# Attention and ELU feed-forward on one core: v by even and odd columns, w_in in eight loads over 128 partitions, and another order of all steps

## The chip, the core and the metric

The kernel runs on one core of one Trainium2 chip. The metric is the device time of one execution in microseconds. Three runs of the kernel before took 332.55, 333.47 and 333.83 us; the median is 333.47 us.

## The reference

Attention over 8 batches, 8 heads, 576 tokens and 64 dimensions, with 16 beacon keys and values ahead of the causal ones, and then a feed-forward layer on the 4,608 tokens (512 to 2,048 to 512) with an ELU between its two products. All inputs and the output are float32.

```python
k_all = np.concatenate([beacon_k, k], axis=2)
v_all = np.concatenate([beacon_v, v], axis=2)
scores = scale * np.matmul(q, k_all.transpose(0, 1, 3, 2))   # causal ones masked, beacons always seen
a = np.exp(scores - scores.max(-1, keepdims=True))
a /= a.sum(-1, keepdims=True) + 1e-09
x = np.matmul(a, v_all)         # then heads side by side: (4608, 512)
h = x @ w_in
g = np.where(h > 0.0, h, np.exp(np.minimum(h, 0.0)) - 1.0)
return g @ w_out
```

## The kernel before

All engines run an order that is written out by hand: the string handed to `run` (L789 to L912) is a list of some 1,500 words such as `S.1.4`, and each word calls one step, which emits its instructions. Within an engine the instructions keep the order of the words; between engines only the data they pass and the buffers they share hold them back, by semaphores. So a step that waits holds up all later steps of its engine. The words are a plan made elsewhere; in the kernel stand only its result and the pools whose buffers it has to respect.

A word's first number is the batch for attention steps and the token tile for feed-forward steps. Tiles 0 and 1 are the first 512 tokens in halves of 256, tiles 2 to 9 have 512 tokens each. The steps, with their engine:

- `warm` and `wm` (PE): dummy matmuls of 512 and 128 columns.
- `lq`, `lv`, `wi`, `wo`, `lk` (POOL): loads of q and k (L136), v (L144 and L149), w_in (L161), w_out (L165), and of q and k of later batches to scratch in DRAM (L759). They change the type on the way and are issued by POOL. The program has eight semaphores for POOL's loads and gives them out in turn, so that a load waits for the landing of the eighth load before it.
- `lp` (POOL, L775 and L776): fills the beacon columns and the padding of a key buffer for batches 3 and later. These buffers are the ones from which batches 1 and 2 are transposed. `lt` (SP, L766) is the DMA transpose from scratch for the same batches.
- `T` (PE, L265): transposes of q and k for batches 0 to 2 into PSUM; `cq` (DVE) and `ck` (ACT) copy them out (L278); `cb` (DVE) puts in the beacon keys.
- `S` (PE, L319): scores of 512 columns (416 for batch 0) and two heads; `x` (ACT, L334): their exp into `et`; `m` (DVE, L339): the causal mask; `D` (DVE, L392): sums for the denominators.
- `L` (PE, L376 and L418): column sums of the exps, with a matrix of ones; `n` (ACT, L433 and L436): Ln and Exp that make the reciprocals; `W` (PE, L376): exps times v; `M` (DVE, L470, L480 and L487): product of both into `xT`, the input of the feed-forward layer.
- `F` (PE, L510): first product for 128 of the 2,048 columns (256 for tiles 0 and 1); `e` (ACT, L520), `u` (ACT, L526, or DVE with `.v`, L528), `k` (DVE, L538), or `r` and `g` (DVE): the ELU into `gt`.
- `G` (PE, L559) with `o` and `s`: second product of tiles 0 and 1. From tile 2 on the second product is made with seven products of halves in place of eight: `wt` and `Z` (DVE, L580) make the sums, `Q` (PE, L626) a part of the 112 matmuls of a tile, `J` (ACT or DVE) takes them out and SP stores them. Tiles 8 and 9 make 12 of the 16 parts of the first product in the same way (`H`, `X`, `P`, `K`, `E`, `U`, `V`).

PSUM has three tags of two buffers each: `hps` (F, P, and the transposes of batch 0), `S` (scores, transposes of batches 1 and 2, L and W, two banks each), and `ops` (G, Q, and L and W of batch 0's first 256 queries). A step that takes a buffer waits until the buffer's last reader is done.

In `quad` (L367 and on) the weights of a W matmul are 32 columns of one head of v, and four heads stand side by side in the 128 columns of PE. `half` says which 32 of the 64 columns. So partition 32*i + d of `xT` holds, for head i of a group of four, column d (half 0) or 32 + d (half 1), and w_in must have its rows in the same order. That is why `load_wi` (L157) makes one load for each head: 32 partitions, two rows each, 1,024 columns; eight loads for each half of the columns.

Of the kernel before, what the change touches and what calls it, by code (L numbers as in the profile page):

```python
# [17 lines left out]
def kernel(  # L18
# [135 lines left out]
    wi_v = moe_w_in.rearrange("(g i t d) f -> i d g t f", i=4, t=2, d=32)  # L154
    wo_v = moe_w_out.rearrange("(f p) m -> p f m", p=P)

    def load_wi(c):  # L157
        f_ = slice(DF // 2 * c, DF // 2 * (c + 1))
        for g in range(2):
            for i in range(4):  # L160
                nc.gpsimd.dma_start(  # L161
                    out=w_in16[32 * i:32 * (i + 1), 2 * g:2 * g + 2, f_], in_=wi_v[i, :, g, :, f_])
# [204 lines left out]
    def quad(b, g, qa, qe, t, half, first):  # L367


        v16 = None if half is None else vt[b]  # L370
        pcs = [(j, max(a, qa), min(e, qe), c + max(a, qa) - a) for (j, a, e, c) in lays[b]
               if max(a, qa) < min(e, qe)]
        for n, (j, a, e, c) in enumerate(pcs):
            for i in range(4):
# [1 line left out]
                nc.tensor.matmul(  # L376
                    out=t[32 * i:32 * (i + 1), a - qa:e - qa],
                    lhsT=ones[0:kc[j], :] if half is None else v16[0:kc[j], j, h, 32 * half:32 * (half + 1)],
                    rhs=et(b, p)[0:kc[j], i % 2, c:c + e - a],
                    start=(first and n == 0), stop=(n == len(pcs) - 1), skip_group_check=True)  # L380
# [415 lines left out]
    m.0.3.2 x.0.2.1 S.0.3.1 m.0.0.0 x.0.3.1 m.0.3.0 cb.1.2 lq.1.0.0.4 S.0.0.3 x.0.0.3 L.0.A
    T.1.0.0 n.0.A cq.1.0.0 cb.1.3 T.1.1.0 ck.1.1.0 wm.4 m.0.0.3 S.1.2 lv.0.2 lv.0.0.1 W.0.A.1
    M.0.A.1 x.1.2 S.1.1 x.1.1 W.0.A.0 M.0.A.0 S.0.3.3 x.0.3.3 S.0.2.2 wi.0 F.0.2 x.0.2.2 S.1.5
    S.1.0 m.0.1.2 e.0.2 m.0.2.2 u.0.2 k.0.2 x.1.5 x.1.0 m.0.0.2 lv.0.3.4 F.0.0 m.0.3.3 F.0.1
    cb.2.0 e.0.1 u.0.1.v k.0.1 L.0.B n.0.B W.0.B.0 M.0.B.0 e.0.0 W.0.B.1 M.0.B.1 u.0.0 k.0.0  # L800
    F.0.3 e.0.3 S.1.4 u.0.3.v k.0.3 x.1.4 wi.1 F.0.4 e.0.4 S.1.3 x.1.3 F.1.1 e.1.1 lq.1.0.4.8
    u.1.1 cb.2.1 T.1.2.0 T.1.3.0 u.0.4.v k.0.4 cq.1.3.0 F.0.5 m.1.1.0 ck.1.2.0 e.0.5 F.1.7
    u.0.5.v k.1.1 e.1.7 u.1.7.v k.1.7 S.1.8 x.1.8 S.1.6 x.1.6 wo.0 G.0.1.0 F.0.6 e.0.6 u.0.6.v
    k.0.6 S.1.7 x.1.7 F.1.4 e.1.4 S.1.11 u.1.4.v x.1.11 F.1.5 e.1.5 k.1.4 S.1.12 x.1.12 S.1.9
    x.1.9 wo.2 u.1.5.v k.1.5 F.1.3 S.1.10 F.1.2 lq.2.0.4.8 T.2.2.0 m.1.0.0 x.1.10 cq.2.2.0
    lq.2.0.0.4 m.1.1.1 m.1.0.1 cb.2.2 e.1.3 T.2.1.0 ck.2.1.0 G.0.0.0 wo.1 u.1.3 T.2.3.0 m.1.3.0
    m.1.2.1 T.2.0.0 ck.2.0.0 cq.2.3.0 lv.1.0.1 G.0.0.1 F.0.7 lk.3.1 S.2.1 e.1.2 H.1.1 m.1.3.1
# [133 lines left out]
```

## Time and profile before

| what | value |
|---|---|
| median of three runs | 333.47 us |
| span of the profiled execution, first to last instruction | 331.3 us |
| granted TensorE clock | 0.998 |
| PE, DVE, ACT busy | 97%, 88%, 83% of the span |
| POOL busy | 27%, nearly all in the first 200 us |
| loads of w_in | 16 of 128 KB, median 5.5 us from issue to landing |
| DMA issues by POOL, SP and ACT | 94, 60 and 5 |

The profile is that of one execution; its span is 2.2 us under the median of the runs, which measure a little more than from the first to the last instruction. PE busy is the time with a matmul somewhere in PE; as matmuls overlap, a busy PE need not be at its peak. KB of a load are those that it writes, after the change of type. "Idle before" is the time that an engine sat idle ahead of an instruction, with what ended it.

### The profile page before, as it was taken

To read this page: it belongs to the slowest core of one execution; us is meant where nothing else is said; L and a number is where in the kernel's file an instruction comes from. 1 tells how busy PE (TensorE), PEld (TensorE's weight loads), DVE (VectorE), ACT (ScalarE), POOL (GpSimd) and SP (SyncE) were. 2 spreads that over 40 slices of the span, in tenths; PEclk is the share of its full clock that TensorE was granted. 3 is DMA by queue.
4 is the path that set the end of the run, shared out by engine and by line. 5 is a ranking of instruction groups with operands and counts; after the bars stand their busy time and mean duration, and the time that the engine had idled before them with its cause. 6 is when DMAs were issued, how large, how long until landed. Compare 5 with 4: busy or idle time off the path is not lost.

```text
span 331.3 us, 8764 instructions
## 1 busy us (share of the span) xinstructions
PE 322.5 (97%) x3576; PEld 208.3 (63%) x3576; DVE 291.8 (88%) x614; ACT 274.9 (83%) x446; POOL 88.3 (27%) x117
## 2 busy tenths in 40 slices
PE   8889999999999999999999999999999999999995
PEld 4657765544446565655665665556656788788784
DVE  3866888989998999999999789999999999999962
ACT  1898998699999998998898789996889687798730
POOL 8888266664008805000830050000000000000000
PEclk9999999999999999999999999999999999999999
DMA  9999999999989998952999098101100011011112
GB/s 114 172 169 182 199 191 172 160 148 156 164 193 69 172 164 135 97 117 60 104 192 153 3 110 133 33 0 34 66 32 3 33 65 34 32 65 34 64 66 95
DMA packets 129113, 34.66 MB, mean 105 GB/s; under 512 B 112944, under 2 KB 127536, under 8 KB 129072
## 3 DMA queue, kind: packets, MB, share of 16 engines
q0 software_dynamic: 94944, 18.49, 67.9%
q1 hardware_dynamic: 33408, 15.34, 20.8%
q8 instruction: 28, 0.46, 0.6%
q10 hardware_dynamic: 720, 0.26, 0.3%
q14 instruction: 13, 0.11, 0.1%
HBM read 37.22 MB, written 15.34 MB: 159 GB/s over the span
## 4 chain that ended last, share of the span: by engine, by line
PE 80%; DMA 10%; POOL 4%; ACT 2%; DVE 1%; issue 1%; DVEq 0%; POOLq 0%
PE hps L510 27%; PE ops L626 27%; DMA v<-in_v_dram 6%; PE sc L319 6%; PE ut L376 6%; PE hps L696 6%; PE ops L559 4%; DMA w_out<-in_moe_w_out_dram 3%; PE sx L626 2%; PE lt L376 1%; POOL qst L136 1%; POOL kst L136 1%; ACT et L334 1%; PE lt L418 1%; POOL v L149 1%
## 5 line engine op out<-in xcount | busy, mean ns | idle before, releaser
L510 PE MATMUL hps<-xT,w_in 128*128 128x512 f16 (+1 forms) x544 | 118.6, 355 | 0.3 <-DVE gt L550 0.2
L334 ACT ACTIVATE et<-sc 128x1024 f16<-128x1024 f32 (+2 forms) x114 | 103.6, 979 | 10.9 <-PE sc L319 10.8
L520 ACT ACTIVATE e<-hps 128x512 f32<-128x512 f32 x120 | 73.2, 617 | 18.9 <-PE hps L510 17.8
L626 PEld LDWEIGHTS <-gt 128*128 128x128 f16 x768 | 73.4, 98 | 19.9 <-issue 3.7
L538 DVE SCALAR_TENSOR_TENSOR gt<-e,r 128x512 f16<-128x512 f32 x112 | 75.4, 684 | 5.7 <-ACT r L526 5.0
L510 PEld LDWEIGHTS <-w_in 128*128 128x128 f16 x544 | 50.6, 98 | 41.9 <-issue 3.9
L526 ACT ACTIVATE r<-hps 128x512 f16<-128x512 f32 x88 | 54.3, 619 | 0.0
L626 PE MATMUL ops<-w_out,gt 128*128 128x256 f16 x368 | 48.0, 273 | 0.0
L626 PE MATMUL ops<-wt,gt 128*128 128x256 f16 x352 | 47.3, 273 | 0.0
L149 POOL DMA_DIRECT2D v<-in_v_dram x40 | 34.7, 914 | 10.6 <-DMA scr<-in_q_dram 3.6
L339 DVE TENSOR_TENSOR et<-et,triu 128x512 f16<-128x512 f16 (+4 forms) x108 | 31.6, 331 | 2.1 <-ACT et L334 2.1
L580 DVE TENSOR_TENSOR gt<-gt 128x1024 f16<-128x1024 f16 x48 | 32.2, 683 | 0.6 <-PE ops L626 0.3
L376 PEld LDWEIGHTS <-v 128*32 128x32 f16 (+1 forms) x800 | 17.4, 96 | 11.6 <-issue 4.2
L392 DVE TENSOR_TENSOR qk<-qk,et 128x672 f16<-128x672 f16 (+2 forms) x66 | 23.3, 367 | 0.5
L376 PE MATMUL ut<-et,v 128*32 128x464 f16 (+3 forms) x560 | 21.3, 296 | 0.0
L144 POOL DMA_DIRECT2D v<-in_beacon_v_dram x8 | 4.8, 595 | 61.8 <-PE lt L376 48.6
L528 DVE TENSOR_SCALAR r<-hps 128x512 f16<-128x512 f32 x24 | 16.4, 685 | 3.1 <-ACT e L520 2.8
L470 DVE TENSOR_TENSOR xT<-ut,rl 128x672 f16<-128x672 f32 (+12 forms) x26 | 16.4, 669 | 1.2 <-PE ut L376 0.7
L642 DVE TENSOR_TENSOR osb<-ops,sm 128x512 f32<-128x512 f32 x23 | 15.7, 682 | 1.0 <-PE ops L626 1.0
L559 PE MATMUL ops<-w_out,gt 128*128 128x512 f16 x64 | 16.4, 381 | 0.0
L735 DVE SCALAR_TENSOR_TENSOR gt<-e,r 128x512 f16<-128x512 f32 x24 | 15.9, 681 | 0.0
L706 ACT COPY kst<-hps 128x512 f32<-128x512 f32 x18 | 10.6, 588 | 5.9 <-PE hps L696 5.8
(113 smaller groups left out, 417.9 us busy)
## 6 DMA issues: line engine op xcount, KB each, us to landing
out_dram<-osb SPq DMA_DIRECT2D x35, 256.0 KB, 2.4
v<-in_v_dram POOLq DMA_DIRECT2D x24, 128.0 KB, 8.4
scr<-in_k_dram POOLq DMA_DIRECT2D x5, 576.0 KB, 12.8
scr<-in_q_dram POOLq DMA_DIRECT2D x5, 576.0 KB, 12.6
w_in<-in_moe_w_in_dram POOLq DMA_DIRECT2D x16, 128.0 KB, 5.5
w_out<-in_moe_w_out_dram POOLq DMA_DIRECT2D x4, 512.0 KB, 10.4
qst<-in_q_dram POOLq DMA_DIRECT2D x4, 288.0 KB, 9.4
kst<-in_k_dram POOLq DMA_DIRECT2D x4, 288.0 KB, 10.0
```

Source lines behind the costliest of these rows:

```text
L149: nc.gpsimd.dma_start(out=vt[b][r0:r0 + n, j, :, :], in_=v[b, :, ilo[j]:ilo[j] + n, :].rearrange("h s d -> s h d"),)
L334: nc.scalar.activation(out=ets[b, d][:, :, a - EC2 * d:e - EC2 * d], in_=sc[b, g][:, :, a - c0:e - c0], func=AFT.Exp, bias=0.0, scale=SCALE)
L339: nc.vector.tensor_tensor(out=o, in0=o, in1=i, op=ALU.mult)
L376: nc.tensor.matmul(out=t[32 * i:32 * (i + 1), a - qa:e - qa], lhsT=ones[0:kc[j], :] if half is None else v16[0:kc[j], j, h, 32 * half:32 * ...
L392: (nc.vector if eng == "v" else nc.gpsimd).tensor_tensor(out=o, in0=t[0:rows, :, a:e] if n == 0 else o, in1=t[0:rows, :, col:col + e - a], ...
L510: nc.tensor.matmul(out=h[:, n_, :], lhsT=w_in16[:, cc, P * fc:P * (fc + 1)], rhs=xt[k][:, cc, a - TT * k:e - TT * k], start=(cc == 0), sto ...
L520: nc.scalar.activation(out=eb[t, i], in_=flat(hp[t, i]), func=AFT.Exp, bias=0.0, scale=1.0)
L526: nc.scalar.activation(out=rb[t, i], in_=flat(hp[t, i]), func=AFT.Relu, bias=0.0, scale=1.0)
L538: nc.vector.scalar_tensor_tensor(out=half(t, i), in0=eb[t, i], scalar=1.0, in1=rb[t, i], op0=ALU.subtract, op1=ALU.min)
L559: nc.tensor.matmul(out=ob[t, tb_], lhsT=gt[:, fc, P * tb_:P * (tb_ + 1)], rhs=w_out16[:, fc, :], start=(fc == 0), stop=(fc == NFC - 1))
L580: (nc.vector if eng == "v" else nc.gpsimd).tensor_tensor(out=o_, in0=a_, in1=b_, op=op_)
L626: nc.tensor.matmul(out=xy[t, n_][:, qd, :], lhsT=lw[:, P * qd:P * (qd + 1)], rhs=wt_[:, c, :], start=(first and c == 0 and (qd == 0 or (t, ...
```

## The change

Three things are changed, and nothing else.

1. `half` now picks the even or the odd columns of v's head (every second element of a row of 64) and not the first or the last 32. Partition 32*i + d of `xT` then holds columns 2d and 2d + 1 of head i.
2. w_in's rows are then in the order in which they lie in memory, two rows for each partition, and one load fills 128 partitions: 128 x 2 x 512, 256 KB. `wi.c` loads a quarter of the 2,048 columns in two loads, and `wi.0` to `wi.3` take the place of `wi.0` and `wi.1`: eight loads in place of sixteen.
3. The string has the same words (but for `wi.2` and `wi.3`) in another order, on all engines. `P` takes its PSUM buffers at whichever of its phases comes first.

```diff
-    wi_v = moe_w_in.rearrange("(g i t d) f -> i d g t f", i=4, t=2, d=32)
+    wi_v = moe_w_in.rearrange("(g p t) f -> g p t f", g=2, t=2)
...
     def load_wi(c):
-        f_ = slice(DF // 2 * c, DF // 2 * (c + 1))
+        f_ = slice(DF // 4 * c, DF // 4 * (c + 1))
         for g in range(2):
-            for i in range(4):
-                nc.gpsimd.dma_start(
-                    out=w_in16[32 * i:32 * (i + 1), 2 * g:2 * g + 2, f_], in_=wi_v[i, :, g, :, f_])
+            nc.gpsimd.dma_start(out=w_in16[:, 2 * g:2 * g + 2, f_], in_=wi_v[g, :, :, f_])
...
-                    lhsT=ones[0:kc[j], :] if half is None else v16[0:kc[j], j, h, 32 * half:32 * (half + 1)],
+                    lhsT=ones[0:kc[j], :] if half is None else v16[0:kc[j], j, h, half:D:2],
...
-        if ph == 0:
+        if (t, g, 0) not in hx:
```

The order of the words up to the first steps of batch 2, engine by engine, where the prediction speaks of it:

```diff
 POOL
-lq.0.0.0.4 lq.0.1.0.4 ident lq.0.0.4.8 lq.0.1.4.8 tri lq.1.0.0.4 lv.0.2 lv.0.0.1 wi.0 lv.0.3.4 wi.1 lq.1.0.4.8 wo.0 wo.2 lq.2.0.4.8 lq.2.0.0.4 wo.1 lv.1.0.1 lk.3.1 lv.1.2.3.4 wo.3 lk.3.0 lk.6.0 lp.3.1 lp.4.0
+lq.0.0.0.4 lq.0.1.0.4 ident lq.0.0.4.8 lq.0.1.4.8 tri lq.1.0.0.4 lv.0.0.1 lv.0.2 wi.1 wi.0 lv.0.3.4 wi.2 lq.1.0.4.8 wi.3 wo.0 lp.3.0 lq.2.0.4.8 lq.2.0.0.4 lv.1.0.1 wo.1 lv.1.2.3.4 lp.4.0 wo.2 lk.3.0 lk.3.1 wo.3
 PE
-warm.4 warm.4 warm.4 wm.4 wm.4 T.0.0.0 bt wm.4 wm.4 wm.4 T.0.1.0 S.0.0.0 T.0.1.1 S.0.1.0 ... S.0.3.1 S.0.0.3 L.0.A T.1.0.0 T.1.1.0 wm.4 S.1.2 W.0.A.1 S.1.1 W.0.A.0 S.0.3.3 S.0.2.2 F.0.2 S.1.5 S.1.0 F.0.0 F.0.1 L.0.B W.0.B.0 W.0.B.1 F.0.3 S.1.4 F.0.4 S.1.3 F.1.1 T.1.2.0 T.1.3.0 F.0.5 F.1.7 ... F.1.2 T.2.2.0 T.2.1.0 G.0.0.0 T.2.3.0 T.2.0.0
+wm.4 wm.4 warm.4 wm.4 wm.4 wm.4 warm.4 bt T.0.1.0 warm.4 T.0.0.0 S.0.1.0 T.0.1.1 S.0.0.0 ... S.0.1.2 L.0.A S.0.2.2 wm.4 S.0.2.3 wm.4 T.1.0.0 T.1.1.0 W.0.A.0 W.0.A.1 S.0.3.1 S.0.3.3 S.0.3.2 F.0.2 S.1.3 S.1.1 F.0.3 F.0.1 L.0.B W.0.B.1 S.1.5 F.0.0 F.0.4 S.1.0 W.0.B.0 S.1.4 F.0.5 S.1.2 T.1.2.0 F.1.1 T.1.3.0 ... F.0.7 S.1.11 T.2.3.0 F.0.6 T.2.2.0 T.2.0.0 F.1.7 T.2.1.0
 ACT
-x.0.0.0 x.0.1.0 ... x.0.3.1 x.0.0.3 n.0.A ck.1.1.0 x.1.2 x.1.1 x.0.3.3 x.0.2.2 e.0.2 u.0.2 x.1.5 x.1.0 e.0.1 n.0.B e.0.0 u.0.0 e.0.3 x.1.4
+x.0.1.0 x.0.0.0 ... x.0.2.2 x.0.2.3 n.0.A ck.1.1.0 x.0.3.1 x.0.3.3 x.0.3.2 e.0.2 u.0.2 x.1.3 x.1.1 e.0.3 e.0.1 n.0.B x.1.5 e.0.0 u.0.0 x.1.0
```

From there on the order differs in the same manner up to the last tile: the same kinds of steps alternate on each engine, in other pairings. The last words are nearly the same: the products of tile 9 with its stores.

More of the change, by code (lines that the diff above doesn't have):

```diff
@@ L796 @@
[L796 to L807, printed above, removed]
@@ L910 @@
[L910 to L911 removed]
+    wm.4 wm.4 warm.4 lq.0.0.0.4 lq.0.1.0.4 wm.4 ident wm.4 wm.4 warm.4 lq.0.0.4.8 bt bk T.0.1.0
+    cq.0.1.0 warm.4 cb.0.0 cb.0.1 T.0.0.0 S.0.1.0 T.0.1.1 cq.0.0.0 S.0.0.0 cq.0.1.1 x.0.1.0
+    T.0.0.1 x.0.0.0 S.0.1.1 wm.4 x.0.1.1 S.0.1.3 x.0.1.3 cq.0.0.1 T.0.2.0 lq.0.1.4.8 T.0.3.0 tri
+    m.0.1.0 cb.0.3 S.0.0.1 cq.0.2.0 S.0.0.2 cb.0.2 cq.0.3.0 x.0.0.1 T.0.2.1 x.0.0.2 S.0.3.0
@@ new lines @@
+    lq.1.0.4.8 u.0.3.v u.0.1.v k.0.1 S.1.5 x.1.5 F.0.0 M.0.B.1 e.0.0 F.0.4 u.0.0 k.0.0 S.1.0
+    H.1.1 W.0.B.0 x.1.0 e.0.4 M.0.B.0 m.1.0.0 S.1.4 F.0.5 x.1.4 u.0.4.v e.0.5 S.1.2 cb.2.1
+    T.1.2.0 u.0.5.v k.0.5 x.1.2 wi.3 wo.0 F.1.1 T.1.3.0 cb.2.0 ck.1.2.0 e.1.1 cq.1.3.0 u.1.1
+    S.1.6 F.1.4 S.1.9 x.1.6 k.1.1 F.1.6 x.1.9 S.1.7 e.1.4 x.1.7 S.1.8 m.1.1.1 k.0.3 u.1.4.v
+    k.0.4 G.0.0.0 lp.3.0 F.1.5 m.1.0.1 x.1.8 S.1.12 cb.2.2 e.1.6 S.1.10 G.0.1.0 m.1.2.1 u.1.6.v
+    e.1.5 m.1.2.0 F.0.7 x.1.12 k.1.6 u.1.5.v lq.2.0.4.8 x.1.10 S.1.11 cb.2.3 u.0.7 k.1.4
@@ new lines @@
+    M.3.0.1 Q.2.63.70 S.4.6 M.3.0.0 u.3.0 S.4.5 J.2.3 F.3.5 m.3.2.0 s.1.1 u.3.2.v k.3.0 F.3.1
+    Z.2.4.1 Q.2.70.77 Q.2.77.84 x.4.5 m.3.3.1 e.3.5 u.3.5 m.4.0.0 Q.2.84.91 k.3.5 F.3.12 u.3.1
+    e.3.1 m.3.2.1 D.3.3.0 D.3.3.1 S.4.7 x.4.6 lp.5.1 D.3.2.0 lk.7.0 D.3.2.1 D.3.2.2 k.3.2
+    D.3.2.3 S.4.4 lv.6 D.3.3.2 e.3.12 u.3.12 x.4.7 x.4.4 k.3.1 F.3.11 F.3.3 J.2.4 D.3.3.3 k.3.12
+    u.3.11 W.3.1 L.3.1 e.3.11 k.3.11 u.3.3 m.4.1.0 D.4.1.0 e.3.3 F.3.4 k.3.3 n.3.1 F.3.10
+    m.4.2.0 e.3.10 lv.4 Q.2.91.98 u.3.10 M.3.1.0 Q.2.98.105 M.3.1.1 k.3.10 u.3.4 F.3.13 u.3.13
@@ new lines @@
+    u.4.15 Z.3.4.1 S.5.11 m.5.1.0 D.5.0.1 D.5.0.2 F.4.14 x.6.4 Q.3.84.91 S.5.10 k.4.15 H.2.0
+    x.5.11 e.4.14 u.4.14 S.5.6 Q.3.91.98 Q.3.98.105 x.5.6 D.5.1.0 x.5.10 lk.7.1 lt.6.1 J.3.5
+    u.4.11 Z.4.1.0 k.4.13 F.5.12 k.4.14 e.5.12 D.5.0.3 e.4.11 u.5.12.v S.6.1 Z.4.3.1 k.4.11
+    S.5.8 x.5.8 m.5.2.1 m.5.1.1 D.5.1.1 Q.3.105.112 Z.4.1.1 Q.4.0.7 x.6.1 F.5.15 S.6.0 D.5.1.2
+    D.5.1.3 S.6.3 Q.4.7.14 e.5.15 F.5.7 x.6.0 x.6.3 L.5.0 m.5.2.0 k.5.12 u.5.15 W.5.0 F.5.9
+    n.5.0 M.5.0.1 J.3.6 M.5.0.0 m.5.3.0 e.5.7 Q.4.14.21 J.4.0 u.5.7.v Q.4.21.28 S.6.2 m.6.0.0
@@ new lines @@
+    u.5.9 S.5.12 lt.7.1 H.4.1 e.5.9 k.5.7 Z.4.2.0 x.6.2 Z.4.2.1 k.5.9 x.5.12 F.5.11 e.5.11
+    u.5.11 k.5.11 F.5.14 H.4.0 Q.4.28.35 S.6.8 S.6.5 D.5.3.0 u.5.14 e.5.14 k.5.15 J.4.1 x.6.5
+    m.5.3.1 F.5.10 x.6.8 F.5.5 D.5.3.1 Q.4.35.42 e.5.10 Q.4.42.49 u.5.5 J.4.2 S.6.9 S.6.10 e.5.5
+    u.5.10.v k.5.10 Q.4.49.56 D.5.3.2 Z.4.4.1 x.6.10 F.5.8 u.5.8 D.5.2.0 Q.4.56.63 D.5.3.3 x.6.9
+    F.5.3 m.6.1.0 S.6.6 Z.4.4.0 e.5.8 lt.7.0 x.6.6 D.5.2.1 k.5.14 D.5.2.2 W.5.1 D.5.2.3 k.5.8
+    L.5.1 u.5.3 e.5.3 Q.4.63.70 lp.7.0 F.5.0 k.5.3 m.6.1.1 F.5.4 n.5.1 k.5.5 m.6.0.1 e.5.0
@@ new lines @@
+    M.6.0.0 D.6.2.1 F.6.8 M.6.0.1 k.6.3 e.6.8 D.6.2.2 S.7.12 S.7.1 k.6.5 r.6.8 F.6.6 x.7.1
+    x.7.12 e.6.6 g.6.8 Q.5.14.21 Z.5.1.1 Z.5.2.0 F.6.9 S.7.0 S.7.5 r.6.6 e.6.9 r.6.9 J.5.0 g.6.6
+    D.6.3.0 D.6.2.3 g.6.9 x.7.0 k.6.2 m.7.0.0 Q.5.21.28 Q.5.28.35 J.5.1 x.7.5 F.6.0 Z.5.2.1
+    S.7.11 D.6.3.1 u.6.0 e.6.0 S.7.6 F.6.13 F.6.14 D.6.3.2 x.7.6 W.6.1 e.6.13 x.7.11 r.6.13
+    D.6.3.3 g.6.13 e.6.14 m.7.1.0 L.6.1 r.6.14 F.6.7 e.6.7 m.7.0.1 u.6.7 D.7.0.0 Q.5.35.42
+    Q.5.42.49 F.6.12 D.7.0.1 n.6.1 g.6.14 e.6.12 M.6.1.1 u.6.12 F.6.10 Q.5.49.56 D.7.1.0 m.7.1.1
@@ new lines @@
+    J.5.2 k.6.12 F.6.1 M.6.1.0 k.6.0 Q.5.56.63 u.6.10 S.7.9 Z.5.4.1 S.7.8 Z.5.4.0 e.6.10
+    Q.5.63.70 Q.5.70.77 e.6.1 x.7.8 r.6.1 F.6.4 k.6.7 J.5.3 e.6.4 g.6.1 Q.5.77.84 D.7.0.2 F.7.1
+    x.7.9 u.6.4 Q.5.84.91 S.7.10 D.7.0.3 e.7.1 k.6.10 Z.6.3.1 J.5.4 u.7.1 x.7.10 k.6.4 m.7.2.1
+    S.7.7 F.6.15 D.7.1.1 F.6.11 e.6.15 m.7.3.1 Q.5.91.98 e.6.11 u.6.15 D.7.1.2 D.7.1.3 L.7.0
+    Q.5.98.105 Z.6.3.0 F.7.12 k.6.15 u.7.12 J.5.5 m.7.3.0 Q.5.105.112 e.7.12 x.7.7 Q.6.0.7
+    r.6.11 g.6.11 Z.6.1.0 J.5.6 Z.6.1.1 F.7.6 D.7.3.0 e.7.6 k.7.12 m.7.2.0 F.7.2 D.7.3.1 D.7.2.0
@@ new lines @@
+    D.7.2.1 u.7.6 k.7.6 D.7.3.2 e.7.2 Q.6.7.14 u.7.2 D.7.3.3 Q.6.14.21 F.7.15 Z.6.2.0 e.7.15
+    Q.6.21.28 u.7.15 D.7.2.2 n.7.0 F.7.7 k.7.1 F.7.8 k.7.15 e.7.7 J.6.0 M.7.0.0 r.7.7 e.7.8
+    D.7.2.3 g.7.7 u.7.8 k.7.8 W.7.1 L.7.1 F.7.13 u.7.13 e.7.13 F.7.5 Q.6.28.35 Z.6.4.0 F.7.0
+    u.7.5 Z.6.2.1 k.7.2 J.6.1 k.7.13 Q.6.35.42 e.7.5 F.7.10 k.7.5 u.7.0 n.7.1 M.7.1.1 Z.6.4.1
+    e.7.0 e.7.10 Q.6.42.49 Q.6.56.63 F.7.14 u.7.10 e.7.14 k.7.10 u.7.14 M.7.1.0 F.7.3 H.3.0
+    k.7.0 X.8.1 u.7.3 Q.6.49.56 X.8.2 F.7.4 J.6.2.v e.7.3 F.7.9 k.7.3 e.7.4 k.7.14 u.7.4
@@ new lines @@
+    Q.6.63.70 u.7.9 X.8.4 e.7.9 F.7.11 P.8.0.0 e.7.11 Q.6.70.77 J.6.3 Q.6.77.84 u.7.11 H.3.2
+    K.8.0.0 X.8.3 P.8.0.1 P.8.0.2 k.7.9 k.7.4 K.8.0.1 Q.6.84.91 K.8.0.2 J.6.4 E.8.0.1 k.7.11
+    P.8.0.3 K.8.0.3 P.8.0.4 Q.6.91.98 K.8.0.4 U.8.0.1 P.8.0.5 P.8.0.6 E.8.0.6 H.3.1 E.8.0.4
+    J.6.5 K.8.0.5 Q.6.98.105 Q.6.105.112 F.8.15 Z.7.3.0 U.8.0.6 J.6.6 u.8.15 P.8.1.0 Z.7.3.1
+    V.8.0.6 e.8.15 Z.7.1.1 Q.7.0.7 Q.7.7.14 U.8.0.4.v P.8.1.1 K.8.1.0 P.8.1.2 Q.7.14.21 k.8.15
+    V.8.0.1 E.8.0.5 K.8.1.1 P.8.1.3 K.8.1.2 P.8.1.4 K.8.1.3 V.8.0.4 E.8.1.1 U.8.0.5.v Q.7.21.28
@@ new lines @@
+    E.9.1.6 V.9.0.6 Q.8.35.42 J.8.1 U.9.1.6 V.9.1.6 F.9.14 U.9.1.4 E.9.1.4 V.9.1.4 e.9.14
+    Z.8.4.0 F.9.12 u.9.14 u.9.12 e.9.12 U.9.1.5.v Q.8.42.49 Q.8.49.56 J.8.2 P.9.2.0 k.9.12
+    P.9.2.1 K.9.2.0 K.9.2.1 U.9.2.1 E.9.1.5 Z.8.4.1 Q.8.56.63 P.9.2.2 k.9.14 E.9.2.1 V.9.1.5
+    Q.8.63.70 J.8.3 P.9.2.3 K.9.2.2 Q.8.70.77 Q.8.77.84 P.9.2.4 K.9.2.3 P.9.2.5 Z.9.3.0 Z.9.1.0
+    Q.8.84.91 K.9.2.4 K.9.2.5 J.8.4 E.9.2.5 P.9.2.6 V.9.2.1 U.9.2.5.v V.9.2.5 E.9.2.6 F.9.15
+    U.9.2.6 V.9.2.6 u.9.15 Q.8.91.98 F.9.13 e.9.15 U.9.2.4 k.9.15 Q.8.98.105 J.8.5 u.9.13
@@ L912 @@
+    E.9.2.4 Q.9.0.7 Q.8.105.112 V.9.2.4 Z.9.3.1 e.9.13 J.8.6 k.9.13 Z.9.1.1 Q.9.7.14 Q.9.14.21
+    Z.9.2.0 J.9.0 Q.9.21.28 Z.9.2.1 Q.9.28.35 Q.9.35.42 J.9.1 Q.9.42.49 Z.9.4.0 J.9.2 Q.9.49.56
+    Q.9.56.63 Q.9.63.70 Q.9.70.77 J.9.3 Z.9.4.1 Q.9.77.84 Q.9.84.91 J.9.4 Q.9.91.98 J.9.5
+    Q.9.98.105 Q.9.105.112 Jh.9.0 Jh.9.1
     """)
```

170 lines of the change are left out of this document (60 added, 110 removed).

## Prediction

> **What bounds the kernel now.** I read the page first: busy shares, slices, chain.
>
> ```profile
> span 331.3 us, 8764 instructions
> PE 322.5 (97%) x3576; PEld 208.3 (63%) x3576; DVE 291.8 (88%) x614; ACT 274.9 (83%) x446; POOL 88.3 (27%) x117
> DMA  9999999999989998952999098101100011011112
> PE 80%; DMA 10%; POOL 4%; ACT 2%; DVE 1%; issue 1%; DVEq 0%; POOLq 0%
> ```
>
> PE is the bound on average, and DMA is busy in nearly every slice of the first half. The chain puts 14% on DMA and POOL, all of it early. Whether that is time that could be won, only the stages tell, so I read busy time by stretch next (the numbers after the stretch are its length, then PE, PEld, DVE, ACT and POOL busy, clock, DMA share, GB/s moved).
>
> ```profile
> 0.00:20.00 20.00, 16.68 (x264) 10.42 (x266) 11.70 (x40) 11.72 (x15) 16.12 (x31) 1.00 1.29 151
> 20.00:60.00 40.00, 38.93 (x700) 26.41 (x694) 31.32 (x64) 35.84 (x52) 26.62 (x38) 1.00 1.53 181
> 60.00:320.00 260.00, 259.68 (x2562) 165.43 (x2562) 246.66 (x508) 225.82 (x378) 45.60 (x51) 1.00 0.80 90
> ```
>
> From 60 us to 320 us PE shows 0.32 us of idle time. That stretch is PE work and nothing else, and the same matmuls remain in it. What can be won lies ahead of 60 us: 3.3 us of visible idle in the first 20 us and 1.1 us in the next 40, 4.4 us in all, although some PE work there is dummy matmuls. So the DMA links of the chain lie beside a PE that is over 97% busy from 20 us on: DMA sets when stages may start, not the rate.
>
> In the first 20 us the rate is ACT's:
>
> ```profile
> 9.20 1.62 ACT L334 ACTIVATE et<-sc 128x832 f16<-128x832 f32 x2 [7.12 <-PE sc L319]
> 11.18 9.19 ACT L334 ACTIVATE et<-sc 128x832 f16<-128x832 f32 x12 [0.35 <-PE sc L319]
> 20.16 0.69 ACT L433 ACTIVATE rl<-la 128x512 f32<-128x512 f32 x1
> 20.88 0.63 ACT L436 ACTIVATE rl<-rl 128x512 f32<-128x512 f32 x1
> 21.42 1.10 ACT L278 COPY qk<-tp 128x1152 bf16<-128x1152 bf16 x1
> 22.42 3.45 ACT L334 ACTIVATE et<-sc 128x1024 f16<-128x1024 f32 x4
> 25.78 0.60 ACT L520 ACTIVATE e<-hps 128x512 f32<-128x512 f32 x1
> 26.27 0.59 ACT L526 ACTIVATE r<-hps 128x512 f16<-128x512 f32 x1
> ```
>
> After the first exp at 9.20 ACT pauses only for 0.35 us. One batch-0 exp takes 9.19/12 = 0.77 us, one expert exp or relu 26.27 - 25.78 = 0.49 us.
>
> **The change part by part.** The steps are the same ones on both sides: 3,576 weight loads and matmuls, 445 ACT and 614 DVE operations. Only `wi` comes four times instead of twice, and their order differs. So no engine gains or loses work, and the sum is made of waits.
>
> *Start, up to the end of F.0.0.* Before, 14 exps stand ahead of the normaliser n.0.A, and the two W.0.A steps are split by S.1.1:
>
> ```profile
> 22.99 0.84 PE L376 MATMUL ua<-et,v 128*32 128x256 f16 x24
> ...
> 24.70 1.05 PE L510 MATMUL hps<-xT,w_in 128*128 128x256 f16 x8
> ...
> 29.18 2.57 PE L376 MATMUL ub<-et,v 128*32 128x320 f16 x80
> 31.68 1.05 PE L510 MATMUL hps<-xT,w_in 128*128 128x256 f16 x8
> 32.66 0.39 PE L319 MATMUL sc<-qk 64*128 64x192 bf16 x4
> 32.98 1.05 PE L510 MATMUL hps<-xT,w_in 128*128 128x256 f16 x8
> ```
> ```profile
> 23.89 0.69 DVE L480 TENSOR_TENSOR xT<-ua,rl 128x512 f16<-128x512 f32 x1 [0.32 <-PE ua L376]
> ```
> ```profile
> 12.26 6.96 DMA v<-in_v_dram
> ```
>
> The second row is F.0.2, the first real expert step. After, 13 exps stand ahead of n.0.A, so it starts about 0.8 us sooner (19.4 us), is done at 20.7, and the two W.0.A stand side by side as soon as v is there (12.26 + 6.96 = 19.2 us). The two M steps then end at 20.7 + 2 x 0.69 = 22.1 us, and F.0.2 starts at 22.1 to 22.4 against 24.70, if its quarter of w_in is there.
>
> That lead is not kept whole, because ACT is still full. After n.0.A it does: copy 1.0 (21.7), three exps at 0.77 (24.0), e and u of F.0.2 (25.0), two exps of 1,024 columns at (3.45 - 2 x 0.77)/2 = 0.95 (26.9), two e (27.9), the Ln of n.0.B at 0.7 (28.6). S.1.5 needs the PSUM buffer that this Ln reads, so it goes at 28.6, and F.0.0 behind it runs from 28.9 to 29.9. By then PE has done 16 batch-0 and 3 batch-1 score steps, 4 F, 3 W, 2 L. Before, at 31.68, it had done one score step (0.32 us) and one W.0.B (2.57/2 = 1.28) more and one F (0.98) less, that is 0.6 us more: the same amount stood at 31.1 us. Lead 1.2 us. Bounds: nothing (ACT gives it back later) and the 4.4 us of idle time; I take **-1.2 us**, from rows.
>
> *w_in in wide loads.* Sixteen loads of 32 partitions become eight of 128, the same bytes in runs half as long. The trace has no wide w_in load; it has wide w_out loads. In the first stretch below mainly w_in lands, in the second w_out, q and k:
>
> ```profile
> 20.00:30.00 10.00, 9.28 (x218) 6.67 (x215) 5.67 (x15) 9.76 (x14) 8.57 (x15) 1.00 1.17 166
> 30.00:40.00 10.00, 9.88 (x173) 7.18 (x162) 8.99 (x16) 8.61 (x14) 4.97 (x8) 1.00 1.24 195
> ```
>
> At 166 to 195 GB/s the first quarter (512 KB) needs 2.7 to 3.2 us behind v: it is there at 21.9 to 22.4 us, just in time for F.0.2. The whole w_in (2 MB) takes 10.8 to 12.6 us either way. POOL saves 8 issues of 0.54 us, which lie beside the DMA pipe: nothing. POOL also waits for a landing 8 loads back before each issue, and larger loads mean more bytes in flight:
>
> ```profile
> 16.25 1.58 POOL L161 DMA_DIRECT2D w_in<-in_moe_w_in_dram x3 [1.28 <-DMA kst<-in_k_dram]
> ```
>
> Such waits go, but the pipe is full behind them: 0, with bounds 0 and -1.3. [...]
>
> *Strided weights.* The 800 loads of v weights read every second element. No strided load is in the trace; the nearest rows differ in width and source:
>
> ```profile
> L376 PEld LDWEIGHTS <-v 128*32 128x32 f16 x672 | 14.5, 96 | 10.5 <-issue 4.2 <-DMA v<-in_v_dram 0.2
> L319 PEld LDWEIGHTS <-kst 64*128 64x128 bf16 x160 | 5.4, 94 | 6.8 <-issue 6.1 <-PE ops L626 0.2
> L265 PEld LDWEIGHTS <-qst 96*64 96x64 bf16 x96 | 2.7, 109 | 1.0 <-issue 0.8
> ```
>
> 32 and 128 columns cost the same (96 and 94 ns), so the pattern should cost nothing. Upper bound: 13 ns more each (109 - 96), wholly exposed, four side by side: 800 x 13/4 = 2.6 us. A gain has no source. I take 0.
>
> *Mode changes on PE.* A lone score step between two F takes 32.98 - 32.66 = 0.32 us; two side by side take 0.55 (start to the matmul behind them):
>
> ```profile
> 38.55 0.39 PE L319 MATMUL sc<-hi 64*128 64x272 bf16 x4
> ...
> 39.10 1.04 PE L559 MATMUL ops<-w_out,gt 128*128 128x512 f16 x4
> ```
>
> So one change of tiling pair costs about 0.32 - 0.275 = 0.05 us. The order of both programs has 176 changes of tile shape before and 168 after: **-0.4 us** (bounds 0 and -0.8). [...]
>
> *What the new order may add after 36 us.* In the new order the same engines are as densely planned, and the trace cannot show its waits. Visible PE idle after 60 us is 0.3 us before; I allow the same again, **+0.3 us**, with bounds -0.3 and +4 (the second rival). New queueing: lp.3.0, a POOL memset of a buffer that T.1.3.0 reads, is moved from behind all loads of batches 1 and 2 to ahead of them. Behind it wait q and k of batch 2, v of batch 1 and three quarters of w_out.
>
> Sum: 331.3 - 1.2 - 0.4 + 0.3 = 330.0 us of span. The median shown, 333.47, is 2.2 us over the profiled span, so **332.2 us** (-0.4%).
>
> **The rivals.**
>
> *Slower: the POOL queue stands still behind lp.3.0.* Before, that memset ran late:
>
> ```profile
> 57.16 0.69 POOL L775 MEMSET kst<- 128x96 bf16 x1
> ...
> 36.06 0.53 PE L265 MATMUL tp<-identb,kst 96*64 96x96 bf16 x12
> ...
> 46.78 0.45 PE L265 MATMUL tp<-identb,qst 96*64 96x96 bf16 x12
> ```
> ```profile
> qst<-in_q_dram POOLq DMA_DIRECT2D x4, 288.0 KB, 9.4
> kst<-in_k_dram POOLq DMA_DIRECT2D x4, 288.0 KB, 10.0
> qst<-in_q_dram POOLq DMA_DIRECT2D x2, 128.0 KB, 4.5
> ```
>
> After, it waits for T.1.3.0 (36.06 + 0.53 before; about 36.5 with the lead). By then the DMA pipe has drained: 512 KB fewer stand ahead than before. The k load of batch 2 is issued at 37.2 us, and T.2.3.0 wants it when T.2.2.0 stood before, at 46.78, less the lead and about 1 us of work fewer ahead: 44.3 us. An empty pipe lands 128 KB in 4.5 us and so 288 KB in perhaps 6: hidden. A landing as slow as the 10.0 of the full pipe comes at 47.2: 2.9 us of PE idle, the lead gone too as everything behind is late, so 335 to 337, say 336. It decides from 7.1 us of landing time on. Against it: the queue is empty then.
>
> [...]
>
> *Nothing: ACT takes the lead back.* ACT was 90% busy (35.84 of 40) from 20 to 60 us; the lead is only worth something if ACT runs as far ahead. Then only order noise remains: 333.5.
>
> **How the numbers follow.** Half a per cent (1.7 us) is about what a measurement of this kernel can tell from no change: faster means under 331.8, slower over 335.1. Forecast 332.2, own range 331.0 to 333.4, chance 0.42 (a third of it under 331.8: 0.14). Faster rival 0.18. Nothing 0.10. Slower rival, and a strided load that costs (334.8), 0.30. So faster 0.32, same 0.38, slower 0.30. The range reaches from 329.0 to 336.8, which leaves out the far ends of both rivals.
>
> **What would show it.** Start: F.0.2's matmuls at 22 to 23 us, n.0.A's Ln at 19.4; F.0.0 ends near 30. If F.0.2 waits on w_in beyond 23, the loads are slower than w_out's. [...] Strides: the mean of the v weight loads stays at 96 ns and a W step takes as long as before. lp.3.0: a POOL memset near 36.5 us and idle POOL ahead of it; PE idle at the T.2 steps near 44 us for the slower rival. After 60 us, PE idle of over 1.5 us would make the +0.3 wrong. The prediction fails most likely in this last term, as it is a sum over hundreds of waits that no row shows.

## The result and the profile after

The kernel after takes 331.9 us (median of 20 runs, 330.88 to 333.55), the kernel before 333.28 us in the same series (20 runs, 331.97 to 335.55). The ratio is 0.9962, with a 95% interval of 0.9946 to 0.9978: 1.3 us faster. The ratios below leave out a single execution, one of quarter_narrow's, which took 336.2 us at a mean clock of 0.989. The profiled execution after has a span of 330.0 us.

First the head of the page after (span, busy time of the engines, DMA share in 40 slices, shares of the chain that ended last):

```profile
span 330.0 us, 8747 instructions
PE 321.8 (98%) x3576; PEld 209.5 (63%) x3576; DVE 291.2 (88%) x614; ACT 275.0 (83%) x446; POOL 85.0 (26%) x109
DMA  9999799999999989998995591010200011010122
PE 82%; ACT 11%; DVE 3%; issue 1%; DMA 1%; ACTq 0%; DVEq 0%
```

The engines do the same work as before. DMA and POOL are all but gone from the chain (14% before, 1% now) and ACT has 11% in place of 2%: in the chain the start now hangs on the exps, not on loads.

Then busy time by stretch (length, PE, PEld, DVE, ACT, POOL, clock, DMA share, GB/s):

```profile
0.00:20.00 20.00, 17.95 (x312) 11.91 (x315) 12.00 (x39) 12.26 (x16) 17.65 (x31) 1.00 1.29 148
20.00:60.00 40.00, 38.40 (x696) 26.06 (x689) 31.78 (x69) 36.51 (x54) 20.54 (x28) 1.00 1.48 169
60.00:320.00 260.00, 259.44 (x2531) 166.42 (x2529) 245.61 (x505) 225.31 (x376) 46.78 (x51) 1.00 0.85 93
20.00:30.00 10.00, 8.73 (x191) 6.32 (x184) 6.40 (x18) 9.32 (x14) 3.53 (x5) 1.00 1.42 195
```

PE's visible idle time falls from 3.32 to 2.05 us in the first stretch, and rises from 1.07 to 1.60 us in the second and from 0.32 to 0.56 us in the third. The rise in the second stretch (0.53 us) is one stop of 0.76 us. PE in order of time, after:

```profile
21.31 0.21 PE L317 MATMUL sc<-hi 64*128 64x128 bf16 x1 [0.29 <-ACT qk L276]
22.29 0.53 PE L317 MATMUL sc<-hi 64*128 64x128 bf16 x9 [0.76 <-issue]
22.75 1.05 PE L508 MATMUL hps<-xT,w_in 128*128 128x256 f16 x8
...
29.11 1.92 PE L508 MATMUL hps<-xT,w_in 128*128 128x256 f16 x16
```

The first two rows are the score steps S.0.3.3 and S.0.3.2; the third row is F.0.2, 1.95 us sooner than before (24.70). The last row is F.0.0 with F.0.4 behind it; F.0.0 ends 0.98 us into it, at 30.1 us. PE stands still for 0.76 us inside S.0.3.3, and "issue" says that the profile shows nothing it waited for. ACT pays for it: S.0.3.3's exp comes late (last row).

```profile
18.91 0.68 ACT L431 ACTIVATE rl<-la 128x512 f32<-128x512 f32 x1
20.16 1.10 ACT L276 COPY qk<-tp 128x1152 bf16<-128x1152 bf16 x1
21.16 0.87 ACT L332 ACTIVATE et<-sc 128x832 f16<-128x832 f32 x1
22.67 1.62 ACT L332 ACTIVATE et<-sc 128x832 f16<-128x832 f32 x2 [0.65 <-PE sc L317]
```

Last, the rows of the two edits: the weight loads from v, the loads of w_in, and the memset of lp.3.0 with T.2.3.0, the step that needs the loads queued behind it.

```profile
L374 PEld LDWEIGHTS <-v 128*32 128x32 f16 (+1 forms) x800 | 17.6, 96 | 10.2 <-issue 2.8 <-DVE xT L468 0.2
w_in<-in_moe_w_in_dram POOLq DMA_DIRECT2D x8, 256.0 KB, 9.0
36.15 0.18 POOL L773 MEMSET qst<- 128x96 bf16 x1 [9.55 <-PE tp L263]
44.53 0.45 PE L263 MATMUL tp<-identb,qst 96*64 96x96 bf16 x12 [0.17 <-ACT et L332]
```

A strided weight load takes 96 ns, as a contiguous one did. POOL sits idle for 9.55 us ahead of the memset, and T.2.3.0 does not wait for the loads behind it: it waits 0.17 us, and for ACT.

### The profile page after: what moved, and what is told of

Its sections match the earlier page's. It is cut to its first block, busy times and chain, and to the rows that moved or that the text cites. A ratio compares the mean times of both kernels' runs of the same rounds, so it can differ in the third digit from the quotient of the medians.

```text
span 330.0 us, 8747 instructions
## 1 busy us (share of the span) xinstructions
PE 321.8 (98%) x3576; PEld 209.5 (63%) x3576; DVE 291.2 (88%) x614; ACT 275.0 (83%) x446; POOL 85.0 (26%) x109
## 4 chain that ended last, share of the span: by engine, by line
PE 82%; ACT 11%; DVE 3%; issue 1%; DMA 1%; ACTq 0%; DVEq 0%
PE hps L508 28%; PE ops L624 25%; ACT et L332 7%; PE sc L317 6%; PE hps L694 6%; PE ut L374 6%; PE ops L557 4%; PE sx L624 2%; ACT e L518 2%; PE lt L374 2%; DMA lo<-in_beacon_k_dram 1%; ACT r L524 1%; DVE qk L390 1%; PE lt L416 1%; PE tp L263 1%
## 5 line engine op out<-in xcount | busy, mean ns | idle before, releaser
L332 ACT ACTIVATE et<-sc 128x1024 f16<-128x1024 f32 (+2 forms) x114 | 105.4, 988 | 11.4 <-PE sc L317 10.9
L149 POOL DMA_DIRECT2D v<-in_v_dram x40 | 36.7, 1056 | 5.5 <-issue 4.4
L390 DVE TENSOR_TENSOR qk<-qk,et 128x416 f16<-128x416 f16 (+2 forms) x66 | 23.7, 367 | 0.7
L144 POOL DMA_DIRECT2D v<-in_beacon_v_dram x8 | 6.8, 856 | 63.9 <-PE ops L624 25.5
L624 PE MATMUL ops<-w_out,s 128*128 128x256 f16 x112 | 15.0, 273 | 0.0
```

Of the source, the lines that this page charges most:

```text
L149: nc.gpsimd.dma_start(out=vt[b][r0:r0 + n, j, :, :], in_=v[b, :, ilo[j]:ilo[j] + n, :].rearrange("h s d -> s h d"),)
L332: nc.scalar.activation(out=ets[b, d][:, :, a - EC2 * d:e - EC2 * d], in_=sc[b, g][:, :, a - c0:e - c0], func=AFT.Exp, bias=0.0, scale=SCALE)
L390: (nc.vector if eng == "v" else nc.gpsimd).tensor_tensor(out=o, in0=t[0:rows, :, a:e] if n == 0 else o, in1=t[0:rows, :, col:col + e - a], ...
L624: nc.tensor.matmul(out=xy[t, n_][:, qd, :], lhsT=lw[:, P * qd:P * (qd + 1)], rhs=wt_[:, c, :], start=(first and c == 0 and (qd == 0 or (t, ...
```

## The experiments

The theory was the prediction's: the order brings the gain through its start, and loads and strides bring nothing. The rivals: the wide loads bring it; the order behind the start brings it or costs; POOL's wait costs. Each run is compared with runs of before on its own chip.

**wide_only: the loads and columns without the order.** Code of after, order of before.

```diff
-S.0.2.2 wi.0 F.0.2
+S.0.2.2 wi.1 wi.0 F.0.2
...
-x.1.4 wi.1 F.0.4
+x.1.4 wi.2 wi.3 F.0.4
```

> The order of before with the new loads and the new columns: v by even and odd columns, w_in in eight loads over 128 partitions, the quarter that F.0.2 reads first. Theory of the prediction (the order brings the gain, loads and strides bring nothing): the time of before, 333.3 us, within 0.5 us; F.0.2 again starts after 24 us, because the two W.0.A steps with S.1.1 between them and the score steps ahead of it still stand there. Rival (the wide loads bring the gain): 332.0 us, and 4.5 us of landing time or less for the first 1,024 KB of w_in, against some 5 us before. Rival (strided weights cost): 334 to 336 us and more than 96 ns for a weight load of v.

Measured: 333.28 us against 333.23, ratio 1.0005 (0.9984 to 1.0025). By themselves the new loads and the strides are worth nothing, as predicted. The profiled execution happened to be the slowest of the twelve, 336.26 us. Its PE rows, and the stretch from 27 to 30 us (the clock is the last number but two), show what was special in it:

```profile
23.77 0.49 PE L374 MATMUL ua<-et,v 128*32 128x256 f16 x15
25.41 0.35 PE L374 MATMUL ua<-et,v 128*32 128x256 f16 x9 [1.15 <-issue]
```
```profile
27.00:30.00 3.00, 3.00 (x19) 1.59 (x18) 0.91 (x3) 2.46 (x4) 1.81 (x3) 0.50 1.25 206
```

PE stops for 1.15 us in the middle of a W step, and soon after runs at a clock of 0.50. The other eleven have mean clocks of 0.997 and more.

**order_only: the order without the loads and columns.** Code of before, order of after.

```diff
-wi.1 M.0.A.0 wi.0 lv.0.3.4 wi.2
+wi.0 M.0.A.0 lv.0.3.4 wi.1
...
-wi.3 wo.0 F.1.1
+wo.0 F.1.1
```

> The new order with the columns and the loads of before: eight loads of 32 partitions for each half of w_in, the first half where the new order has its first quarter, the second where it has the third. Theory of the prediction: nearly the time of after. F.0.2 must now wait for a whole half of w_in, which lands 5.2 us behind v (18.3 us), at 23.5 us; so it starts at 23.6 to 23.9 us against 22.75 after, and up to 1.0 us of the lead of 1.2 us goes: 331.9 to 332.9 us. Rival (the wide loads bring the gain whole): 333.3 us or more.

Measured: 334.4 us, ratio 1.0041 (1.0026 to 1.0056): slower than before. The theory's range is missed, and by the number alone the rival's "333.3 us or more" is met; but wide_only has shown that the loads by themselves bring nothing, so the rival does not stand as it was put. The PE rows say what happened, and the stretch behind them what came on top of it in this execution:

```profile
23.26 0.39 PE L510 MATMUL hps<-xT,w_in 128*128 128x256 f16 x2
25.20 1.44 PE L510 MATMUL hps<-xT,w_in 128*128 128x256 f16 x6 [1.54 <-DMA w_in<-in_moe_w_in_dram]
```
```profile
24.00:30.00 6.00, 4.80 (x28) 2.92 (x29) 1.93 (x8) 4.13 (x7) 4.86 (x9) 0.50 1.15 163
```

F.0.2 begins at 23.26 us, runs two of its eight matmuls and then stands until 25.20 us for the rest of the half: 2.45 us later than F.0.2 starts in after (22.75), and the run loses 2.5 us to after. The clock is not needed for that loss: the five executions with a mean clock of 0.997 or more have a median of 334.4 us too. Is it the width of the loads or their unit, a half in place of a quarter? The next two runs ask this.

**half_wide: 128 partitions, but halves.**

```diff
-        f_ = slice(DF // 4 * c, DF // 4 * (c + 1))
+        f_ = slice(DF // 2 * c, DF // 2 * (c + 1))
...
-wi.1 M.0.A.0 wi.0 lv.0.3.4 wi.2
+wi.0 M.0.A.0 lv.0.3.4 wi.1
...
-wi.3 wo.0 F.1.1
+wo.0 F.1.1
```

> After with w_in in four wide loads of 512 KB instead of eight of 256 KB: 128 partitions as after, but F.0.2 has to wait for a whole half of the columns again. The order, the new columns and the width of the loads are those of after. If the unit counts (a quarter is there at 22.2 us, a half at 24.7 to 25.1 us): F.0.2 starts near 25 us, 2.3 us later than after, and the time is 334.2 us (333.7 to 334.7), slower than before, like the run with the new order and the loads of before (334.4). If the width counts: 332 to 332.5 us.

Measured: 333.59 us, ratio 0.9992 (0.9969 to 1.0014), between the two expectations. In the profiled execution (332.14 us) F.0.2 begins at 22.48 us and stands for the half as well, but only for 0.6 us:

```profile
23.46 0.83 PE L508 MATMUL hps<-xT,w_in 128*128 128x256 f16 x6 [0.59 <-DMA w_in<-in_moe_w_in_dram]
```

The twelve executions fall in two groups: six of 331.83 to 333.11 us, with mean clocks of 0.998 to 1.000, and six of 334.08 to 334.92 us with 0.993 to 0.994. That the clock dropped there as in the two stretches above is inferred from the mean alone: 0.005 of 332 us is 1.7 us, nearly the whole distance.

The median of the twelve hides this. The six at the full clock have a median of 332.3 us, where the width theory had it: 0.4 us over after, and against before on their own chip the same ratio, 0.996. order_only, with the same order and the same unit, has 334.4 us at the full clock. There PE goes on with the half at 25.20 us, in half_wide at 23.46. So with wide loads the unit costs 0.4 us or less, and in half of the executions a drop of the clock; with the loads of before it costs 2.5 us. What in the loads makes this difference stays open: those of order_only are narrower and also smaller and more, and POOL issues the eighth of them only at 19.92 us, where half_wide has issued both of its loads by 14.5.

**quarter_narrow: quarters, but 64 partitions.**

```diff
-            nc.gpsimd.dma_start(out=w_in16[:, 2 * g:2 * g + 2, f_], in_=wi_v[g, :, :, f_])
+            for i in range(2):
+                nc.gpsimd.dma_start(
+                    out=w_in16[64 * i:64 * (i + 1), 2 * g:2 * g + 2, f_], in_=wi_v[g, 64 * i:64 * (i + 1), :, f_])
```

> After with each wide load cut in two of 64 partitions: 16 loads of 128 KB, as many and as large as before, still a quarter of the columns at a time. If the unit counts and not the width: the time of after, 331.9 us (331.4 to 332.4), first quarter of w_in there at 21.7 to 22.8 us. If the width counts: 333 us or more, with a first quarter later than 23 us. POOL has eight issues of some 0.55 us more, and would show them as later loads of q and k of batch 1.

Measured: 331.66 us, ratio 0.9933 (0.9908 to 0.9958): the time of after. With a quarter as the unit, loads half as wide (and half as large) cost no time, although the DMA engines move less in the stretch where w_in lands, 167 GB/s against 195 in after:

```profile
20.00:30.00 10.00, 9.30 (x197) 6.99 (x190) 6.90 (x19) 9.97 (x15) 8.55 (x14) 1.00 1.31 167
```

In this profile PE does not stop inside S.0.3.3. It waits for an exp ahead of S.0.3.2, and F.0.2 follows:

```profile
22.13 0.35 PE L319 MATMUL sc<-hi 64*128 64x224 bf16 x4 [0.41 <-ACT et L334]
22.42 1.05 PE L510 MATMUL hps<-xT,w_in 128*128 128x256 f16 x8
```

**start_only and rest_only: the order in two parts.** The first has 141 words of after and then before's order, the second is the mirror of it. The seams:

```diff
 H.1.1 W.0.B.0 x.1.0 e.0.4 M.0.B.0
-m.1.0.0 S.1.4 F.0.5 x.1.4
+wi.3 S.1.2 x.1.2 cb.2.0 S.1.4
```
```diff
 x.1.4 wi.2 wi.3 F.0.4 e.0.4
-S.1.3 x.1.3 F.1.1 e.1.1
+S.1.3 x.1.3 lq.1.0.4.8 H.1.1 m.1.0.0 F.0.5
```

> All of after up to the second M.0.B step (F.0.0 to F.0.4, some 31 us), then all steps that are left in the order of before; loads and columns as after. It has 176 changes of tile shape on PE as before has. Theory of the prediction: it keeps the lead of 1.2 us and not the 0.4 us of the mode changes: 332.1 us (331.6 to 332.6). Rival (the gain comes from the order behind the start): 333.3 us.

> The mirror of the run with the new start: all steps of before up to e.0.4 (some 34 us), then all steps that are left in the order of after; loads and columns as after. 167 changes of tile shape on PE. Theory of the prediction: no lead, 0.4 us less for mode changes and up to 0.3 us more of waits: 333.2 us (332.6 to 333.6). Rival (the order behind the start brings the gain): 332.0 us. Rival (the order behind the start costs, and the lead pays for it): 334 us or more.

Measured: start_only 332.41 us, ratio 0.998 (0.9963 to 0.9997); rest_only 333.0 us, ratio 0.9991 (0.9976 to 1.0007). The start alone brings 0.8 us, the rest alone 0.2, within its error. Both lie where the theory had them; their sum, 1.0 us, is most of the gain of 1.3, and the rest is within the errors. The start lost something at its seam (PE's waits from 30 to 40 us):

```profile
PE sc L317 <- DVE xT L485: 0.7, 1, 0.7
```

**start_long: the seam moved back.** Order of after up to T.1.3.0.

```diff
 x.1.2 wi.3 wo.0 F.1.1 T.1.3.0
-cb.2.0 ck.1.2.0 e.1.1 cq.1.3.0 u.1.1 S.1.6
+cb.2.0 k.0.3 e.1.1 u.1.1 k.0.4 cq.1.3.0
```

> Like the run with the new start, but the order of after is kept until T.1.3.0 (some 36 us) before the order of before takes over. The shorter start lost 0.7 us at its seam, where a score step had to wait for the second M.0.B; here the seam lies behind it. 179 changes of tile shape, 3 more than before. Theory of the prediction: the lead of 1.2 us whole, less 3 x 0.05 to 0.1 us for the changes of shape: 332.2 us (331.7 to 332.7). Rival (the start is worth no more than the 0.8 us of the shorter one, the seam did not matter): 332.4 us or more, PE idle at the seam or not.

Measured: 332.86 us, ratio 0.9983 (0.996 to 1.0005). This misses the theory's range and meets the rival's "332.4 us or more". The new seam has a wait of its own, behind ACT's copy of a transpose, and so the run does not show what the start is worth without one; that it is worth more than the 0.8 us of start_only is not shown.

```profile
PE sc L317 <- ACT hi L276: 0.8, 1, 0.8
```

**mode_same and mode_split: the price of a change of tile shape.** One dummy matmul ahead of each F of tiles 2 to 7, with all 128 rows or with 64 (shown).

```diff
         k = a // TT
+        if 2 <= t <= 7:
+            nc.tensor.matmul(
+                out=h[:, 0, 0:P], lhsT=w_in16[0:64, 0, P * i:P * (i + 1)],
+                rhs=xt[k][0:64, 0, a - TT * k:a - TT * k + P], start=True, stop=True, skip_group_check=True)
```

> After with one dummy matmul of 128 columns ahead of each of the 96 F steps of tiles 2 to 7, with the weights and the input of the F step itself, all 128 rows: no more changes of tile shape (168). The result of the dummy is overwritten. Expected: 96 times some 0.056 us, the step from one matmul of 128 columns to the next, 5.4 us more than after: 337.3 us. It is the base of the next run.

> The same 96 dummy matmuls with 64 rows instead of 128, the tile shape of the score steps: 313 changes of tile shape instead of 168, 145 more. With the price of 0.05 us that the prediction took: 7.2 us more than with 128 rows, 344.5 us. If a change costs nothing: 337.3 us as with 128 rows.

Measured (two executions each): 337.38 us with 128 rows, as expected, and 351.16 us with 64. So 145 changes cost 13.8 us, 0.095 us each, twice the price of the prediction. The same pair of F steps in time, first with 128 rows, then with 64 (start, length):

```profile
115.53 1.03 PE L512 MATMUL hps<-xT,w_in 128*128 128x512 f16 x4
116.39 0.22 PE L506 MATMUL hps<-xT,w_in 128*128 128x128 f16 x1
116.45 1.03 PE L512 MATMUL hps<-xT,w_in 128*128 128x512 f16 x4
```
```profile
118.28 1.04 PE L512 MATMUL hps<-xT,w_in 128*128 128x512 f16 x4
119.25 0.23 PE L506 MATMUL hps<-xT,w_in 64*128 64x128 f16 x1
119.41 1.04 PE L512 MATMUL hps<-xT,w_in 128*128 128x512 f16 x4
```

From F to the dummy it takes 0.86 us without a change and 0.97 with one, from the dummy to the next F 0.06 and 0.16: 0.10 to 0.11 us on the way in, and 0.10 on the way out. The dummy itself takes as long with 64 rows as with 128 (0.23 and 0.22).

**few_dummies: where PE stops.** In wide_only and in after PE stopped at the same place of its stream, though other steps stand there: behind the 351st weight load in the trace (the expectations call it the 350th).

```diff
-wm.4
+warm.1
```

> After with each of the 12 groups of four dummy matmuls of 128 columns replaced by one of 512 columns: the same time on PE, 36 weight loads and 36 matmuls fewer, nothing else moved. In after PE stops for 0.8 us inside S.0.3.3, behind its 350th weight load, with no wait in the program there; the runs with the new order and the loads of before, with the new start, with halves of w_in and with dummies in F stop at the same 350th load, and so does the run with the new loads alone, where that load belongs to W.0.A. If the stop hangs on the place in PE's instruction stream: it moves 36 loads on, into F.0.1 at some 25.5 us, or goes; F.0.2 starts at 22.3 to 22.5 us instead of 22.75, and the time is 331.9 less up to 0.7: 331.2 to 331.6 us. If it hangs on S.0.3.3 or on that moment: a stop of 0.5 to 1 us at 21.3 us as before, and 331.9 us.

Measured: 331.03 us (six runs, 330.83 to 331.21), ratio 0.9911 (0.9885 to 0.9938): faster than both kernels. PE in order of time:

```profile
21.47 0.36 PE L317 MATMUL sc<-hi 64*128 64x128 bf16 x6 [0.29 <-ACT qk L276]
22.52 1.05 PE L508 MATMUL hps<-xT,w_in 128*128 128x256 f16 x8
24.07 2.09 PE L508 MATMUL hps<-xT,w_in 128*128 128x256 f16 x16
28.68 1.92 PE L508 MATMUL hps<-xT,w_in 128*128 128x256 f16 x16
```

S.0.3.3 now runs through, F.0.2 comes at 22.52 us and F.0.0 ends at 28.68 + 0.98 = 29.7. The stop has moved with the stream: that load now lies in F.0.1, in the row of 2.09 us, where the same 16 matmuls took 1.92 us in after; 0.17 us of it is left. That is the expectation for a place in the stream, with a time a little under its 331.2 us.

**before_few: the same in before.** The same replacement in the 12 places of before's order.

> Before with the same replacement of its 12 groups of four dummy matmuls of 128 columns by one of 512 columns. After won 0.6 to 0.9 us by it, since PE reached its 350th load at 21.3 us and stood there until 22.3. Before reaches that load at 23.3 us, inside the second W.0.A, and stands for 0.2 us. If the stop is a wait for something that comes at 22 to 23.5 us whatever the order is: 0 to 0.2 us, 333.0 to 333.3 us, and the new order without the stop is worth 2 us. If fewer dummies help by themselves, whatever stands at that load: 332.6 us.

Measured: 333.45 us against 333.82, ratio 0.9993 (0.9972 to 1.0015). That is the first expectation: fewer dummies by themselves bring nothing. Before reaches the load of the stop 2 us later, at 23.3 us, and stops there for 0.2 us.

**lp_late: POOL's wait taken away.**

```diff
-k.0.4 G.0.0.0 lp.3.0 F.1.5
+k.0.4 G.0.0.0 F.1.5
...
-wo.3 x.2.11
+wo.3 lp.3.0 x.2.11
```

> After with one step of POOL moved back: lp.3.0, the memset that waits for T.1.3.0, stands behind wo.3 instead of ahead of the loads of batch 2. Theory of the prediction (the wait of POOL is hidden): the DMA pipe no longer runs empty between 36.7 and 40 us, q and k of batch 2 land some 5 us sooner, and the time stays that of after, 331.9 us (331.5 to 332.3). Rival (the gate costs something of what the start brings): 331.0 us or less, and less PE idle time between 40 and 60 us than the 0.25 us of after.

Measured: 331.65 us, ratio 0.9939 (0.9917 to 0.996), as after within the error. The DMA engines move 205 GB/s from 30 to 40 us, against 123 in after, and that is worth nothing that can be measured; the rival's 331.0 us is not reached.

## Why the prediction was right, step by step

The forecast of 332.2 us is 0.3 us off, since the median lies 1.9 us over the profiled span and not 2.2 (every execution of after lies 1.7 or 1.8 us over its own span; the 2.2 set the median of three executions against the span of a single one). The span of 330.0 us is exact, and that is luck: three terms were off in size, and their errors cancel.

*Start (-1.2).* The mechanism is right, step by step: n.0.A's Ln at 18.91 us (19.4 predicted), both M.0.A done before F.0.2, ACT full from there on (9.32 of the 10 us from 20 to 30), F.0.0 from 29.1 to 30.1 us (28.9 to 29.9). Measured against the same amount of work at 31.1 us, the lead is 1.0 us. F.0.2 came at 22.75 us and not at 22.1 to 22.4, for two reasons that the prediction did not have. It let F.0.2 follow the second M, which ends at 21.78 us; but S.0.3.3 and S.0.3.2 stand between, and they wait for ACT (0.29 us for a copy and, where PE does not stop, 0.41 for an exp). Without the stop F.0.2 comes at 22.42 us (quarter_narrow) and 22.52 (few_dummies), so the stop adds the last 0.2 to 0.3 us. Without it the lead is 31.1 - 29.7 = 1.4 us (few_dummies). start_only agrees with the sign, not sharply with the size: 0.8 us with a seam that waits 0.7.

*Wide loads (0).* Right for the loads by themselves (wide_only, 1.0005). What the prediction held in half a sentence, "if its quarter of w_in is there", is the part of the edit that counts: with a half as the unit the new order loses its gain in the median, in order_only by a late landing (334.4 us) and in half_wide mostly by the clock (333.59; 332.3 at the full clock). With a quarter, 64 partitions do as well as 128 (quarter_narrow). So the gain belongs neither to the loads nor to the order; the loads alone give 0, the order alone loses 1.2 us, both together win 1.3. The GB/s from 20 to 30 us are 195 against 166 before, and by the 1.0005 of wide_only the faster rival (the wide loads bring the gain) is out.

The speed of wide loads that this rival's chance of 0.18 supposes is shown by no run. What the traces show is this: from 20 to 30 us eight profiles with loads over 128 partitions have 192 to 200 GB/s and the four with 32 or 64 have 161 to 167, so that the wide ones move 1.2 times as much, with several loads in flight (in before POOL issues three loads of w_in in the 1.58 us from 16.25 us on, and none lands in under 4.9 us). The narrow loads are also smaller ones, so width alone is not shown.

*Strides (0).* Right: 96 ns before and after.

*Mode changes (-0.4).* The step that was wrong is "one change of tiling pair costs about 0.32 - 0.275 = 0.05 us". Both times ran from the score step's start to the matmul behind it. They leave out the change ahead of the step, and subtracting half a pair from a single leaves half of the change behind it. The measured price is 0.095 to 0.1 us; eight changes fewer are -0.8 us.

*Waits behind the start (+0.3).* What is left of the -1.3 us after -1.0 and -0.8 is +0.5 us. rest_only says the same in another way: nine changes fewer should bring 0.9 us, and it wins 0.2, so 0.7 us go to waits, with an error of about as much. As idle time only 0.24 us of it are seen (0.56 against 0.32 us after 60 us), well under the 1.5 that would have broken the term. Where the rest is spent stays open.

*POOL behind lp.3.0.* The gate is there as predicted (36.15 us, predicted 36.5), and hidden as forecast: taking it away changes nothing (lp_late).

## What to carry over

An edit to loads and one to the order can be worth nothing each and something together: before pricing a load by its bandwidth, ask which unit the first consumer waits for and when the last load of it is issued, and move both. Where the times of a kernel fall in two groups, read the groups and not their median. The price of a switch is to be taken on both its sides, from the last start ahead of it to the first start behind it. And where a tuned engine stops at "issue", look at what stands at the same place of the instruction stream in another kernel; the same dummy work in fewer instructions brought another 0.6 to 0.9 us here in the new order, and nothing in the old.
